# Chunked attention into a token-mixing MLP on one core: v loaded by pairs of tokens, with the odd tokens copied on chip

## The chip, the core and the metric

The kernel runs on one core of a Trainium2 chip. Five engines work beside each other, each through its own instructions in order: TensorE (PE in the profile; its weight loads are PEld), VectorE (DVE), ScalarE (ACT), GpSimd (POOL) and SyncE (SP), which here only issues transfers. 16 DMA engines move data between the chip's memory and the on-chip buffer SBUF. TensorE writes its results to PSUM, eight banks of 512 float32 per partition. The metric is the device time of one execution in microseconds; lower is better.

## The reference

Attention runs inside chunks of 64 tokens: 8 batches, 8 heads, 576 tokens, head size 64, all float32. Its output, with the heads side by side as 512 features, goes through a token-mixing MLP.

```
s = q_c @ k_c^T / 8 ;  attn = softmax(s) ;  a = attn @ v_c       # per (batch, head, chunk of 64)
x = a.transpose(0, 2, 1, 3).reshape(8, 576, 512)
wq, wk = x @ w_q, x @ w_k                                        # 512 -> 64 each
mixed = (wq @ wk^T / 8) @ x                                      # per batch, over its 576 tokens
out = relu(mixed) @ w_out                                        # float32, (8, 576, 512)
```

Since `(wq @ wk^T) @ x = wq @ (wk^T @ x)`, the kernel computes the 64 by 512 matrix `wk^T @ x` and no 576 by 576 one.

## The kernel before

The work is a list of words, `ORDER`. A loop over it calls one small function for each word, and so every engine's queue holds its instructions in the order of the words. The list is written out by hand or by a planner outside the kernel; nothing reorders it. The framework adds the waits between engines. `@n` names a PSUM bank, `:A`, `:D` or `:P` the engine (ScalarE, VectorE, GpSimd).

**Loading.** q and k are seen as 36 units of 1,024 rows (a row is one token of one head). In a unit, each of the 128 partitions holds 8 rows that follow one another, so a partition gets one run of 512 elements, 2,048 bytes read and 1,024 written as float16. A word `LDk.9_14` loads k of units 9 to 13 to all partitions, and `LDq1.9_14` the quarter of q that goes to the 32 partitions from 32 x 1. Each quarter of q has one of two slots, and the other slot stays zero (`MZ` clears it, once), so that one matmul can mix the two. q and k share a ring of 27 units (`RING`), which later also holds the output tiles on their way out (`held`). `LDv.32` loads all of v of batch 3: partition p holds token p of each 128 tokens, so each token is one run of 64 elements, 256 bytes read and 128 written. All these loads convert to float16 and are issued by GpSimd (lines 134, 142, 146), in the order of the words. `LW` loads `w_out` there too; `LS` loads the small weights through SyncE.

**One unit pair.** `TR` transposes k and q of one or two units in 32 by 32 blocks on VectorE (lines 208 and 212), `SC` computes the scores transposed, k's tokens on the partitions (line 227), and `EX` the exponentials on ScalarE, into `est`. There are 20 such steps: 16 of two units, 4 of one.

**One batch.** `PVb.p`, p = 0, 1, 2, multiplies `est` by v (line 262); v has a column of ones (`MO`), so the sums of the exponentials come with it. `RN` is a reciprocal and a multiplication on VectorE (272, 273), `XT` transposes on TensorE (283) and `XE` copies the result, `PJ` projects to wq and wk (309) and `EP` copies, `DU` duplicates a half on chip, `WT` transposes wk (336) and `EW` copies, `GM` computes `wk^T @ x` (363) and `EG` copies, `MXb.m`, m = 0 to 3, multiplies by wq (381) and `RL` applies the relu. The eight batches are finished in pairs: two batches are nine tiles of 128 tokens, each an `OM` with `w_out` (420), 36 in all, and an `OE` that copies to SBUF (432 on VectorE, 434 on ScalarE). `ST` stores tiles by SyncE (439). The first store waits for the load that `HOLD` names, so that stores don't compete with loads. `ZZn` is n matmuls on constant data (449), placed where TensorE has nothing else.

The functions that the change touches follow, as they were.

Of the kernel before, what the change touches and what calls it, by code (L numbers as in the profile page):

```python
# [17 lines left out]
MU MZ2_5_2:A MO2 LDq1.0_2 ZZ4@0 LDk.2_5 LDq2.0_2 MZ0_2_3:A LDq3.0_2 MZ0_2_0:A MZ2_5_1:D ZZ4@1 MZ2_5_0:A MZ0_2_2:A MO0  # L18
MZ5_9_9:D MO1 LDq0.0_2 LDk.0_2 LS LDq0.2_5 MO3 MZ0_2_1:A LDq3.2_5 LDq1.2_5 LDq2.2_5 MO4 MZ9_14_9:D TR0 ZZ4@0 SC0@0
MZ2_5_3:A LDv.02 TR1 EX0 LDk.5_9 LDq3.5_9 TR2 SC1@2 LDq0.5_9 SC2@0 EX1 LI EX2 LK MZ23_27_9:P PV0.0@0 LDq1.5_9 PV0.2@2  # L20
MZ14_18_9:D RN0.0 RN0.2 LDq2.5_9 PV0.1@4 ZZ4@6 LDq1.9_14 LDv.12 XT0.0@0 LDq3.9_14 XE0.0:A LDq2.9_14 ZZ4@6 RN0.1
MZ18_23_9:P XT0.1@4 TR4 XE0.1:A TR3 SC4@0 PJ0@4 EP0:D SC3@2 WT0@4 EX4 EX3 EW0:A PV1.2@2 PV1.0@0 ZZ4@4 GM0@5 LDq0.9_14
DU0:A RN1.2 PV1.1@2 ZZ4@4 EG0:A RN1.0 MX0.1@0 RN1.1 MX0.3@4 MX0.2@6 RL0.1:A XT1.0@2 RL0.2:A LDk.9_14 XT1.1@0 TR6
XE1.0:A MX0.0@6 LDv.22 ZZ4@2 SC6@2 RL0.0:A XE1.1:A PJ1@0 LW LDk.14_18 EX6 TR5 LDq1.14_18 LDq2.14_18 SC5@2 LDq3.14_18
EP1:A TR7 WT1@0 EX5 EW1:D SC7@6 DU1:D LDq0.14_18 GM1@0 EX7 RL0.3:A PV2.1@6 PV2.2@2 EG1:A LDq1.18_23 RN2.1 OM2@4 OE2:A
MX1.1@0 RN2.2 RL1.1:A MX1.0@6 PV2.0@4 MX1.2@0 RL1.0:A XT2.1@2 RL1.2:A MX1.3@6 RN2.0 XT2.0@4 XE2.1:D XE2.0:A LDq2.18_23
OM0@5 PJ2@3 TR9 OM3@2 LDq3.18_23 SC9@0 EP2:A TR8 EX9 OE0:A OE3:A LDk.18_23 WT2@3 DU2:A OM4@4 EW2:A LDq0.18_23 SC8@0
LDv.32 LDk.23_27 EX8 RL1.3:D OM6@6 OE6:A OE4:D GM2@3 EG2:A LDq0.23_27 OM8@0 MX2.0@3 RL2.0:A TR11 MX2.3@6 RL2.3:D
MX2.1@1 LDq3.23_27 OM5@5 PV3.0@6 RL2.1:A OE8:A PV3.1@0 MX2.2@2 TR12 RN3.0 OE5:A RL2.2:A LDq2.23_27 OM7@5 PV3.2@2
SC11@6 OE7:A SC12@4 EX11 RN3.1 XT3.0@0 LDq1.23_27 RN3.2 LDv.42 OM9@1 TR10 XT3.1@2 XE3.0:A OE9:A OM1@0 XE3.1:A PJ3@2  # L30
EX12 SC10@4 TR14 EP3:A DU3:D EX10 WT3@2 PV4.0@4 EW3:A PV4.1@2 PV4.2@6 LDq3.29_32 GM3@1 LDq1.29_32 OE1:A LDq2.29_32
# [525 lines left out]
```

The loads in their order are these. `LDv.12` is batch 1, all of it (the last digit, 2, means both halves).

```
LDq1.0_2 LDk.2_5 LDq2.0_2 LDq3.0_2 LDq0.0_2 LDk.0_2 LDq0.2_5 LDq3.2_5 LDq1.2_5 LDq2.2_5 LDv.02 LDk.5_9 LDq3.5_9
LDq0.5_9 LDq1.5_9 LDq2.5_9 LDq1.9_14 LDv.12 LDq3.9_14 LDq2.9_14 LDq0.9_14 LDk.9_14 LDv.22 LW LDk.14_18 LDq1.14_18
LDq2.14_18 LDq3.14_18 LDq0.14_18 LDq1.18_23 LDq2.18_23 LDq3.18_23 LDk.18_23 LDq0.18_23 LDv.32 LDk.23_27 LDq0.23_27
LDq3.23_27 LDq2.23_27 LDq1.23_27 LDv.42 LDq3.29_32 LDq1.29_32 LDq2.29_32 LDk.29_32 LDq3.27_29 LDq0.29_32 LDq2.27_29
LDq1.27_29 LDv.52 LDq0.32_36 LDq1.32_36 LDq3.32_36 LDq0.27_29 LDq2.32_36 LDk.27_29 LDk.32_36 LDv.62 LDv.72
```

And the order from the first step that uses v of batch 6:

```
PV6.0@1 OM14@5 EW5:A PV6.1@6 SC18@3 RN6.0 PV6.2@1 OE14:A RN6.1 GM5@5 XT6.0@0 EX18 RN6.2 OM19@3 XT6.1@1 EG5:D LDv.72
DU5:A XE6.0:D MX5.1@4 XE6.1:A MX5.3@6 OM20@0 PJ6@1 RL5.3:A ST0.6 TR19 SC19@6 RL5.1:A OE20:D EP6:D OM18@0 WT6@1 MX5.2@4
EX19 OE19:D EW6:D MX5.0@6 PV7.0@2 GM6@1 OE18:A RL5.2:A PV7.1@4 DU6:D RN7.0 RL5.0:A EG6:D PV7.2@6 OM22@0 RN7.2 OM26@1
OE22:A RN7.1 ST1.0 OM24@0 MX6.0@6 MX6.1@2 XT7.1@4 OE26:A ST0.3 XE7.1:A OE24:D XT7.0@0 OM25@1 RL6.1:D RL6.0:A MX6.3@4
XE7.0:D ST2.0 RL6.3:D ST1.6 OE25:A MX6.2@2 ST1.3 PJ7@6 RL6.2:A EP7:A OM28@2 WT7@6 OM29@7 ST0.0 EW7:D OE29:A DU7:A
OE28:D GM7@6 EG7:A OM27@2 OE27:A MX7.3@6 MX7.0@3 MX7.2@0 RL7.2:A RL7.0:D OM21@5 MX7.1@0 RL7.3:A RL7.1:A OM23@3 ST2.6
OE21:A OM31@0 OE23:D OM32@5 OE31:D OM30@3 OM35@0 ST3.0 OE32:D OE30:A OM34@3 ST2.3 OE34:D ST3.3 ST3.7 OM33@5 OE35:D
OE33:D ST3.8 ST3.6
```

## Time and profile before

| | |
|---|---|
| median of 3 runs | 122.64 us (121.91 to 123.4) |
| the profiled execution | 122.64 us, span of its instructions 120.8 us |
| busy: TensorE / VectorE / ScalarE / GpSimd | 98.1 / 91.9 / 72.3 / 50.2 us |
| loads that GpSimd issues | 47,536 packets, 14.68 MB written |
| read from memory / written to it | 29.62 MB / 9.44 MB |

How to read it: times are from the first instruction. A group's row has the line, the engine, the operation, output and inputs, then busy time and the mean in ns, then the idle time before and what ended it. In the chain of waits each row is a start, a length, and what the end of the kernel hung on then. In a row of a timeline the bracket holds the idle time before and its releaser. The row of a stretch gives its length, busy time and instructions of PE, PEld, DVE, ACT and POOL, the granted clock of TensorE, the mean share of the DMA engines (over 1 where packets overlap) and the GB/s written.

### The profile page before, as it was taken

The numbers are of one execution on the slowest core, as the hardware profiler recorded it, in microseconds if no ns is written. First come the engines' busy times: TensorE is split into PE (matmuls) and PEld (weight loads), VectorE is DVE, ScalarE is ACT, GpSimd is POOL, SyncE is SP. The second block draws the span as 40 slices with busy tenths as digits, with TensorE's granted clock in tenths as the row PEclk, the third lists the DMA queues.
The fourth block names the chain that finished last, engine by engine and source line by source line (L and its number), as shares of the span: only waits on it lengthen the run. The fifth ranks groups of instructions, "written<-read, shape, count | busy, mean of one in ns | idle before, by whom it ended". The sixth has DMA issues, their size and how long they took to land.

```text
span 120.8 us, 3838 instructions
## 1 busy us (share of the span) xinstructions
PE 98.1 (81%) x1664; PEld 55.1 (46%) x1664; DVE 91.9 (76%) x131; ACT 72.3 (60%) x117; POOL 50.2 (42%) x68
## 2 busy tenths in 40 slices
...
GB/s 8 120 196 157 167 205 203 171 179 205 178 175 207 202 203 200 180 172 205 176 172 204 96 157 193 209 171 157 137 156 401 234 351 423 417 123 260 260 362 159
DMA packets 50144, 24.62 MB, mean 204 GB/s; under 512 B 38096, under 2 KB 48336, under 8 KB 50128
## 3 DMA queue, kind: packets, MB, share of 16 engines
q0 software_dynamic: 47536, 14.68, 112.8%
...
q14 instruction: 3, 0.02, 0.0%
HBM read 29.62 MB, written 9.44 MB: 323 GB/s over the span
## 4 chain that ended last, share of the span: by engine, by line
DMA 59%; PE 24%; POOL 7%; issue 5%; DVE 1%; DVEq 0%; POOLq 0%
DMA qk<-in_k_dram 32%; DMA vt<-in_v_dram 27%; PE pb L420 14%; PE pb L363 2%; PE pb L262 2%; POOL qk L146 2%; PE pb L283 2%; POOL qk L153 2%; POOL vt L134 2%; PE pb L381 2%; PE pb L309 2%; DVE qk L432 1%; PE pb L227 1%; POOL qk L142 1%; PE pb L336 1%
## 5 line engine op out<-in xcount | busy, mean ns | idle before, releaser
L420 PE MATMUL pb<-wout,rmx 128*128 128x512 f16 x144 | 35.8, 381 | 0.1
L146 POOL DMA_DIRECT2D qk<-in_q_dram x40 | 22.3, 563 | 20.7 <-DMA vt<-in_v_dram 9.2
L239 ACT ACTIVATE est<-pb 128x1024 f16<-128x1024 f32 (+1 forms) x20 | 18.6, 939 | 12.4 <-PE pb L227 12.4
L273 DVE TENSOR_TENSOR xn<-pb,rec 128x768 f16<-128x768 f32 x24 | 23.0, 958 | 1.0 <-DVE rec L272 0.2
L212 DVE STREAM_TRANSPOSE qT<-qk 128x1024 f32<-128x1024 f32 (+1 forms) x20 | 22.1, 1105 | 1.2 <-DMA qk<-in_q_dram 1.2
L208 DVE STREAM_TRANSPOSE kT<-qk 128x512 f32<-128x512 f32 (+1 forms) x20 | 20.1, 1004 | 2.8 <-DMA qk<-in_k_dram 2.4
L227 PE MATMUL pb<-qT,kT 64*64 64x128 f16 x576 | 12.8, 229 | 8.4 <-DVE qT L212 8.3
L434 ACT COPY qk<-pb 128x512 f32<-128x512 f32 x24 | 13.9, 590 | 8.9 <-PE pb L420 7.9
L420 PEld LDWEIGHTS <-rmx 128*128 128x128 f16 x144 | 13.3, 103 | 12.2 <-issue 0.7
L397 ACT ACTIVATE rmx<-pb 128x576 f16<-128x576 f32 x25 | 15.4, 657 | 2.7 <-PE pb L381 2.6
L134 POOL DMA_DIRECT2D vt<-in_v_dram x8 | 14.8, 1847 | 5.0 <-PE pb L262 3.4
L227 PEld LDWEIGHTS <-kT 64*64 64x64 f16 x576 | 10.2, 112 | 11.2 <-DVE kT L208 4.9
L262 PE MATMUL pb<-vt,est 64*64 64x65 f16 x576 | 8.5, 200 | 6.7 <-DMA vt<-in_v_dram 5.3
L299 ACT COPY xT<-pb 128x768 f32<-128x768 f32 (+1 forms) x13 | 8.5, 651 | 7.7 <-PE pb L283 7.7
L449 PE MATMUL pb<-unit 128*128 128x512 f16 x32 | 11.7, 520 | 1.5 <-DVE unit L465 1.5
L283 PE MATMUL pb<-iden,xn 128*128 128x128 f32 x72 | 11.3, 294 | 0.4 <-DVE xn L273 0.2
L262 PEld LDWEIGHTS <-est 64*64 64x64 f16 x576 | 7.1, 112 | 9.5 <-DMA vt<-in_v_dram 4.4
L272 DVE RECIPROCAL rec<-pb 128x12 f32<-128x12 f32 x24 | 5.4, 227 | 7.4 <-PE pb L262 6.1
L432 DVE COPY qk<-pb 128x512 f32<-128x512 f32 x12 | 8.1, 685 | 3.9 <-PE pb L420 3.7
L283 PEld LDWEIGHTS pb<-iden,xn 128*128 128x128 f32 x72 | 8.8, 151 | 3.4 <-DVE xn L273 1.4
L309 PE MATMUL pb<-xT,wpj 128*128 128x512 f16 (+1 forms) x48 | 9.0, 323 | 0.0
L142 POOL DMA_DIRECT2D qk<-in_k_dram x10 | 7.8, 784 | 2.3 <-DMA qk<-in_k_dram 2.3
...
## 6 DMA issues: line engine op xcount, KB each, us to landing
...
```

What stands on the lines that cost most here:

```text
L134: return nc.gpsimd.dma_start(vt[b % NV][:, lo:hi, 0:D], flat[2][b * H * S : (b + 1) * H * S].rearrange("(c p) d -> p c d", p=P)[:, lo:hi],)
L146: return nc.gpsimd.dma_start(x[rows, 1 + i % 2], runs[0][rows, lo:hi])
L208: nc.vector.transpose(out=kT[x % NQ][:, 0:n].bitcast(F32).rearrange("p u (x r) o -> p u r (x o)", r=R), in_=src[:, 0],)
L212: nc.vector.transpose(out=qT[x % NQ][:, :, 0:n].bitcast(F32).rearrange("p s u r x o -> p s (u r) (x o)"), in_=src[:, 1:3].rearrange("p s u ...
L227: nc.tensor.matmul(ps[CH * o : CH * o + CH, bank + f, at : at + P], lhsT=kT[x % NQ][rows, u, CH * j : CH * j + CH, e], rhs=qT[x % NQ][rows ...
L239: nc.scalar.activation(est[x % NE][:, 0 : 8 * n].rearrange("p m (w r) -> p m w r", r=R), src.rearrange("p (m r w) -> p m w r", r=R, w=R), ...
L262: nc.tensor.matmul(ps[CH * o : CH * o + CH, bank + (n + o) % 2, at : at + D + 1], lhsT=est[x % NE][rows, 4 * size * g + 4 * u + 2 * (j // ...
L273: nc.vector.tensor_tensor(out=xn[b % 3][:, 3 * p : 3 * p + 3].rearrange("p t (f i) d -> p i (t f) d", f=2), in0=xv[:, :, :, 0:D], in1=rec[ ...
L283: nc.tensor.transpose(ps[:, bank + at // 4, P * (at % 4) : P * (at % 4) + P], xn[b % 3][:, i].rearrange("p h c -> p (h c)").bitcast(F32), ...
L397: nc.scalar.activation(dst, src, AF.Relu, scale=scale_moe)
L420: nc.tensor.matmul(ps[:, bank, :], lhsT=c[:, r], rhs=wout[:, i, :], start=(i == 0), stop=(i == NI - 1),)
L434: nc.scalar.copy(os_, ps[:, bank, :])
```

## The change

v of a batch is loaded in two halves, `LDv0.b` and `LDv1.b`: v0 holds the first 64 of each 128 tokens, v1 the others. The 64 tokens are taken as 32 pairs; partition i of 32 gets tokens 2i and 2i + 1 as one run of 128 elements, 512 bytes read and 256 written. `VMb.f` then copies the odd tokens of half f of batch b from these 32 partitions to the next 32, on GpSimd (15 times) or VectorE (once). In each 64 rows of v the even tokens so come first and the odd ones behind, and k's transpose puts its tokens in that order: it is two instructions now, one for each parity. The column of ones moves to the front. v has 3 buffers and not 5.

The ring of q and k has 18 units and not 27, with fewer and longer first and last pieces; the output tiles of the first pair of batches, and three of the second, get a tile of their own (`osb`). `RN` becomes `RC` and `RM`, two words. `ZZ` has 44 matmuls and not 32. The whole order is new. Loads and copies in it:

```
LDq2.0_5 LDq1.0_5 LDq3.0_5 LDq0.0_5 LDq3.5_9 LDk.0_2 LDq1.5_9 LDk.2_5 LDq2.5_9 LDq0.5_9 LDk.5_9 LDv0.0 LDv1.0 LDv1.1
LDv0.1 LDk.9_14 LDq1.9_14 LDq3.9_14 VM0.0:P VM0.1:P VM1.1:P VM1.0:P LDq0.9_14 LDq2.9_14 LDv0.2 LDq1.14_18 LDk.14_18
LDq2.14_18 LDq0.14_18 LDq3.14_18 LDv1.2 LW VM2.0:P LDv0.3 LDv1.3 LDq3.18_23 VM2.1:P LDq1.18_23 LDk.18_23 LDq2.18_23
LDq0.18_23 VM3.1:P LDq1.23_27 LDq3.23_27 VM3.0:D LDv1.4 LDq0.23_27 LDk.23_27 LDq2.23_27 LDv0.4 LDq3.27_32 LDv0.5
LDv1.5 LDq2.27_32 VM4.1:P LDq0.27_32 LDk.27_32 VM4.0:P LDq1.27_32 LDq3.32_36 VM5.0:P VM5.1:P LDq0.32_36 LDv1.6
LDq2.32_36 LDq1.32_36 LDk.32_36 LDv0.6 LDv1.7 VM6.1:P VM6.0:P LDv0.7 VM7.1:P VM7.0:P
```

From the first step that uses v of batch 6:

```
PV6.2@4 RL4.3:A TR18 SC19@2 RC6.2 EG5:A EX19 PV6.1@0 RM6.2 OM20@7 OE15:A RC6.1 SC18@2 RM6.1 PV6.0@5 OM18@4 LDv0.7
DU5:A MX5.0@0 VM7.1:P EX18 OE20:A RC6.0 RM6.0 RL5.0:A MX5.2@2 OE18:D XT6.0@5 VM7.0:P RL5.2:A PV7.0@6 XT6.1@0 XE6.0:A
XE6.1:A ST0.3 PV7.1@2 PV7.2@4 RC7.0 RM7.0 XT7.0@6 RC7.2 PJ6@0 XE7.0:A ST1.0 RC7.1 RM7.2 EP6:A OM19@4 RM7.1 MX5.1@0
MX5.3@2 WT6@5 XT7.1@6 RL5.1:D RL5.3:A EW6:D DU6:A OM22@2 XE7.1:A OM23@5 PJ7@6 OE22:A EP7:A OE19:D DU7:D OM25@2 WT7@6
OE25:A EW7:D ST2.0 OE23:A GM6@7 EG6:A GM7@6 MX6.1@4 RL6.1:A MX6.0@2 EG7:D MX6.3@0 OM21@7 RL6.0:D RL6.3:A ST1.3 OE21:A
MX7.0@2 MX7.3@4 RL7.0:D MX7.2@0 ST0.0 OM26@6 MX7.1@2 RL7.3:A ST2.3 RL7.2:A MX6.2@4 OM24@7 RL7.1:D RL6.2:A OM30@2
OM32@3 OM31@4 OM27@5 ST1.6 OE26:D OM28@6 OE31:A OM29@4 OE24:D OM34@7 OM33@0 OE32:A OE30:D OE27:D OE28:A ST2.6 OE29:A
OE33:D OM35@4 ST3.3 ST3.0 OE34:A ST3.7 OE35:A ST3.6 ST3.8
```

The diff without the order's text:

```diff
 
-HOLD = "v.72"
+HOLD = "v1.7"
 AHEAD = "k.0_2"
 
 
@@ -73,16 +75,16 @@
     NPR = NG // 4
     NI = DM // P
     HS = S // 2
-    VP = 72
+    VP = 130
     VO = D + 2
     R = 8
     NU = B * H * S // (P * R)
-    RING = 27
+    RING = 18
     UNITS = []
     for a in range(0, NU, 9):
         UNITS += [(a, a + 2), (a + 2, a + 4), (a + 4, a + 5), (a + 5, a + 7), (a + 7, a + 9)]
     of_unit = {u: (x, u - lo) for x, (lo, hi) in enumerate(UNITS) for u in range(lo, hi)}
-    NV = 5
+    NV = 3
     NQ = 3
     NE = 5
     scale_attn = 1.0 / math.sqrt(D)
@@ -93,7 +95,7 @@
     ctx.enter_context(tc.manual_schedule())
 
     RD = R * D
-    PIECES = [(0, 2), (2, 5), (5, 9), (9, 14), (14, 18), (18, 23), (23, 27), (27, 29), (29, 32), (32, 36)]
+    PIECES = [(0, 5), (5, 9), (9, 14), (14, 18), (18, 23), (23, 27), (27, 32), (32, 36)]
     qk = sb.tile([P, RING * 3 * RD], F16, name="qk")
 
     def piece(u):
@@ -105,7 +107,7 @@
     kT = [sb.tile([P, 2, 32 * R, 2], F16, name=f"kT{i}") for i in range(NQ)]
     qT = [sb.tile([P, 2, 2, R, 32, 2], F16, name=f"qT{i}") for i in range(NQ)]
     est = [sb.tile([P, 16, CH], F16, name=f"est{i}") for i in range(NE)]
-    rec = [sb.tile([P, 2, 6], F32, name=f"rec{i}") for i in range(3)]
+    rec = [[sb.tile([P, 2, 6], F32, name=f"rec{j}{i}") for i in range(3)] for j in range(2)]
     xn = [sb.tile([P, NPR, 4, D], F16, name=f"xn{i}") for i in range(3)]
     xT = [sb.tile([P, NPR, P, 2], F16, name=f"xT{i}") for i in range(2)]
     wqk = [sb.tile([P, S], F16, name=f"wqk{i}") for i in range(4)]
@@ -117,6 +119,7 @@
     wpj = sb.tile([P, 2, 2, 2 * DH], F16, name="wpj")
     wpl = sb.tile([P, 2, 2 * DH], F16, name="wpl")
     wout = sb.tile([P, NI, DM], F16, name="wout")
+    osb = sb.tile([P, 12 * DM], F32, name="osb")
     ident = sb.tile([P, P], F16, name="ident")
     iden4 = sb.tile([P, P], F32, name="iden4")
     unit = sb.tile([P, 512], F16, name="unit")
@@ -129,11 +132,13 @@
     def load(word):
         it, _, rng = word.partition(".")
         if it[0] == "v":
-            b, f = int(rng[0]), int(rng[1])
-            lo, hi = (0, NG) if f == 2 else (NG // 2 * f, NG // 2 * f + NG // 2)
+            b, f = int(rng), int(it[1])
+            rows = slice(CH * f, CH * f + CH // 2)
             return nc.gpsimd.dma_start(
-                vt[b % NV][:, lo:hi, 0:D],
-                flat[2][b * H * S : (b + 1) * H * S].rearrange("(c p) d -> p c d", p=P)[:, lo:hi],
+                vt[b % NV][rows, :, 2 : 2 + 2 * D],
+                flat[2][b * H * S : (b + 1) * H * S].rearrange(
+                    "(g f i o) d -> f i g (o d)", f=2, i=CH // 2, o=2
+                )[f],
             )
         lo, hi = (int(x) for x in rng.split("_"))
         first, n, x = piece(lo)
@@ -149,8 +154,17 @@
         lo, hi, part = (int(x) for x in word.split("_"))
         n, x = piece(lo)[1:]
         if part == 9:
-            e = nc.vector if eng == "D" else nc.gpsimd
-            e.memset(x[:, n * RD :].bitcast(F32), 0.0)
+            to = x[:, n * RD :].bitcast(F32)
+            if eng == "A":
+                nc.scalar.activation(
+                    to.rearrange("p (u w) -> p u w", w=RD // 2),
+                    unit[:].bitcast(F32)[:, None].broadcast_to([P, 2 * n, RD // 2]),
+                    AF.Copy,
+                    scale=0.0,
+                )
+            else:
+                e = nc.vector if eng == "D" else nc.gpsimd
+                e.memset(to, 0.0)
             return
         rows = slice(32 * part, 32 * part + 32)
         slot = 2 - part % 2
@@ -198,6 +212,15 @@
         make_identity(nc, iden4[:])
         nc.gpsimd.tensor_copy(ident[:], iden4[:])
 
+    def vm(b, f, eng):
+        x = vt[b % NV].bitcast(I32)
+        half = CH // 2
+        lo = CH * f
+        e = nc.vector if eng == "D" else nc.gpsimd
+        e.tensor_copy(
+            x[lo + half : lo + CH, :, 1 : 1 + D // 2], x[lo : lo + half, :, 1 + D // 2 : 1 + D]
+        )
+
     def tr(x):
         lo, hi = UNITS[x]
         first, m, src = piece(lo)
@@ -205,10 +228,11 @@
         src = src.bitcast(F32).rearrange("p (s u r w) -> p s u r w", s=3, u=m, w=32)[
             :, :, lo - first : hi - first
         ]
-        nc.vector.transpose(
-            out=kT[x % NQ][:, 0:n].bitcast(F32).rearrange("p u (x r) o -> p u r (x o)", r=R),
-            in_=src[:, 0],
-        )
+        to = kT[x % NQ][:, 0:n].bitcast(F32)
+        to = to.rearrange("p u (X o l r) z -> p o r (u X) (l z)", X=4, o=2, l=R)
+        of_k = src[:, 0].rearrange("p u (r o) w -> p o r u w", o=2)
+        for o in range(2):
+            nc.vector.transpose(out=to[:, o], in_=of_k[:, o])
         nc.vector.transpose(
             out=qT[x % NQ][:, :, 0:n].bitcast(F32).rearrange("p s u r x o -> p s (u r) (x o)"),
             in_=src[:, 1:3].rearrange("p s u r w -> p s (u r) w"),
@@ -262,18 +286,22 @@
                         nc.tensor.matmul(
                             ps[CH * o : CH * o + CH, bank + (n + o) % 2, at : at + D + 1],
                             lhsT=est[x % NE][rows, 4 * size * g + 4 * u + 2 * (j // 2) + pi],
-                            rhs=vt[b % NV][rows, n // 2, 0 : D + 1],
+                            rhs=vt[b % NV][rows, n // 2, 1 : D + 2],
                             start=True,
                             stop=True,
                         )
 
-    def rn(b, p, bank):
-        xv = ps[:, bank : bank + 2, 0 : 6 * VO].rearrange("p k (n d) -> p k n d", n=6)
-        nc.vector.reciprocal(rec[p][:], xv[:, :, :, D])
+    def values(bank):
+        return ps[:, bank : bank + 2, 0 : 6 * VO].rearrange("p k (n d) -> p k n d", n=6)
+
+    def rc(b, p, bank):
+        nc.vector.reciprocal(rec[b % 2][p][:], values(bank)[:, :, :, 0])
+
+    def rm(b, p, bank):
         nc.vector.tensor_tensor(
             out=xn[b % 3][:, 3 * p : 3 * p + 3].rearrange("p t (f i) d -> p i (t f) d", f=2),
-            in0=xv[:, :, :, 0:D],
-            in1=rec[p][:, :, :, None].broadcast_to([P, 2, 6, D]),
+            in0=values(bank)[:, :, :, 1 : D + 1],
+            in1=rec[b % 2][p][:, :, :, None].broadcast_to([P, 2, 6, D]),
             op=ALU.mult,
         )
 
@@ -325,7 +353,8 @@
         if eng == "A":
             nc.scalar.copy(wq2[b % 4][CH:P], wqk[b % 4][0:CH])
         else:
-            nc.vector.tensor_copy(wq2[b % 4][CH:P], wqk[b % 4][0:CH])
+            e = nc.vector if eng == "D" else nc.gpsimd
+            e.tensor_copy(wq2[b % 4][CH:P], wqk[b % 4][0:CH])
 
     def wt(b, bank):
         t16 = ps[:, bank, :].bitcast(F16)
@@ -397,11 +426,12 @@
             nc.scalar.activation(dst, src, AF.Relu, scale=scale_moe)
 
     of = out.rearrange("b s m -> (b s) m")
-    OB = (9, 15, 21, 0)
-
     def held(pr, at, size):
-        lo = OB[pr] * 3 * RD + at * 2 * DM
-        return qk[:, lo : lo + size * 2 * DM].bitcast(F32)
+        if pr == 0 or pr == 1 and at < 3:
+            lo = at * DM + pr * NCH * DM
+            return osb[:, lo : lo + size * DM]
+        lo = {1: -3, 2: 6, 3: 15}[pr] + at
+        return qk[:, lo * 2 * DM : (lo + size) * 2 * DM].bitcast(F32)
 
     GROUPS = [[3, 3, 3], [3, 3, 3], [3, 3, 3], [3, 3, 1, 1, 1]]
 
@@ -465,7 +495,7 @@
             nc.vector.memset(unit[:], 1.0)
             continue
         if kind == "MO":
-            nc.vector.memset(vt[int(rest)][:, :, D : D + 1], 1.0)
+            nc.vector.memset(vt[int(rest)][:, :, 1:2], 1.0)
             continue
         if kind == "LW":
             weights()
@@ -488,12 +518,16 @@
             tr(n)
         elif kind == "SC":
             sc(n, banks["SC", n, 0])
+        elif kind == "VM":
+            vm(n, x, eng)
         elif kind == "EX":
             ex(n, banks["SC", n, 0])
         elif kind == "PV":
             pv(n, x, banks["PV", n, x])
-        elif kind == "RN":
-            rn(n, x, banks["PV", n, x])
+        elif kind == "RC":
+            rc(n, x, banks["PV", n, x])
+        elif kind == "RM":
+            rm(n, x, banks["PV", n, x])
         elif kind == "XT":
             xt(n, x, banks["XT", n, x])
         elif kind == "XE":
```

56 lines of the change are left out of this document (29 added, 27 removed).

## The prediction

> **What bounds the kernel now.** I read the page first, then the chain of waits in order of time, then stretches of the run, the GpSimd timeline and the groups by shape.
>
> ```profile
> span 120.8 us, 3838 instructions
> PE 98.1 (81%) x1664; PEld 55.1 (46%) x1664; DVE 91.9 (76%) x131; ACT 72.3 (60%) x117; POOL 50.2 (42%) x68
> ...
> GB/s 8 120 196 157 167 205 203 171 179 205 178 175 207 202 203 200 180 172 205 176 172 204 96 157 193 209 171 157 137 156 401 234 351 423 417 123 260 260 362 159
> ...
> q0 software_dynamic: 47536, 14.68, 112.8%
> ...
> DMA 59%; PE 24%; POOL 7%; issue 5%; DVE 1%; DVEq 0%; POOLq 0%
> ```
>
> The chain is 59% transfers, and nearly all the rest is TensorE. In order of time:
>
> ```profile
> 27.52 14.76 DMA qk<-in_k_dram
> ...
> 42.57 7.56 DMA qk<-in_k_dram
> ...
> 50.42 14.26 DMA vt<-in_v_dram
> ...
> 74.92 10.25 DMA vt<-in_v_dram
> ...
> 85.21 0.38 PE pb L262 x24
> ...
> 86.57 0.31 PE pb L262 x23
> ...
> 87.46 1.09 issue
> ...
> 92.94 1.02 PE pb L309 x8
> 93.97 0.58 PE pb L227 x29
> ...
> 100.84 1.13 PE pb L283 x9
> ...
> 102.84 0.35 PE pb L381 x4
> 103.19 1.13 PE pb L309 x8
> ...
> 105.19 0.37 PE pb L336 x6
> ...
> 106.53 0.79 PE pb L363 x10
> ...
> 110.04 5.31 PE pb L420 x24
> 115.35 0.02 issue
> 115.37 1.29 DVE qk L432 x2
> ```
>
> Loads set the pace until v of batch 6 lands at 85.17. From its first matmul, 85.21, TensorE runs to 115.35 with 1.09 idle, so 29.05 us of work. In the written order PV6.0 to the end is 6 PV, 2 pairs of units of SC, 4 XT, 2 PJ, 2 WT, 3 GM, 12 MX and 19 OM. At the rows' prices (PV 0.34, between its two rows; SC 0.58; XT 1.13 a pair; PJ 1.08, the mean of its two rows; WT 0.37; GM 0.79; MX 0.35; OM 5.31/6 = 0.885) this is 31.75. Steps overlap at their ends, so I scale every sum of this kind by 29.05/31.75 = 0.915.
>
> So a release at time T of a step with work W behind it ends TensorE no earlier than T + W. For PV6.0 that is 85.21 + 29.05 = 114.3, and the real end is 1.1 later. Earlier releases have slack:
>
> ```profile
> 28.28 0.58 PE L262 MATMUL pb<-vt,est 64*64 64x65 f16 x48 [1.12 <-DMA vt<-in_v_dram]
> 28.80 1.04 PE L449 MATMUL pb<-unit 128*128 128x512 f16 x4
> ```
>
> PV1.2 starts at 28.28 with 85.5 x 0.915 = 78.3 behind it (21 PV, 13.5 SC, 14 XT, 7 PJ, 7 WT, 8 GM, 32 MX, 36 OM, and 12 matmuls of ZZ at 0.26): 106.6. v of batch 4 lands at 64.7 (50.42 + 14.26) with 52.1 x 0.915 = 47.7 behind PV4.0: 112.4. So the bound rises from load to load: transfers are slower than the work they feed, and the last ones set the end. After TensorE come 5.45 us of copies, the last stores and the finish. The profiled execution took 122.64 us, 1.84 over its span, and is the median of the three runs.
>
> **Transfers.** Two stretches, the columns ending in the granted clock, DMA share and GB/s written:
>
> ```profile
> 42.50:48.00 5.50, 5.43 (x67) 3.15 (x66) 5.30 (x8) 2.27 (x5) 5.43 (x7) 1.00 1.24 201
> 80.00:84.00 4.00, 4.00 (x56) 1.89 (x55) 3.62 (x6) 3.75 (x7) 0.00 (x0) 1.00 2.43 158
> ```
>
> The first holds only q and k, packets of 1,024 B written; the second only v, packets of 128 B. A unit of q or of k (131,072 B) costs 0.65 us, wout 2.6, a batch of v (589,824 B) 3.73. Per packet that is 5.09 ns and 0.81 ns. A line through both gives 1.42 ns at 256 B, so a batch of v in 2,304 packets costs 3.27, a half-batch load 1.64. The bounds are 1.87 (no faster per byte) and 1.47 (as fast as q). I take 1.64, the line through both rows; the saving is 8 x 0.46 = 3.7 us of transfer.
>
> A rule that speaks against the change: the Trainium skill, "SBUF — State Buffer", section "Door 1: The DMA port swizzle", says that 32 partitions from 0 reach 8 of 16 ports, with 189 GB/s measured at 1 MiB against 328 for all; the new v loads write 32 partitions each. By that page's figure a half (294,912 B) would take an estimated 1.56 us, not more than my 1.64, so the rule alone would not undo the gain. The row of 42.5 to 48 is the case in point: from k's landing at 42.3 seven q loads of 32 partitions each are next in the queue, and 201 GB/s were written. So 32 partitions are no limit at the 180 GB/s that 1.64 us means.
>
> When a load lands is the sum of the loads ahead of it in the order plus an offset for start, the weights' transfers, latency and stalls. Batch 4 of v: 54 units 35.1, wout 2.6, five batches 18.7, sum 56.4; it landed at 64.7, offset 8.3. Batch 1: 19.25 units and two batches, 20.0, 28.28: 8.3 too. Batch 6: 75.5, offset 9.7. I use 8.3.
>
> **GpSimd.** It issues all these loads in order, and now also copies.
>
> ```profile
> 1.30 0.66 POOL L146 DMA_DIRECT2D qk<-in_q_dram  x1 [0.86 <-POOLq L541]
> ...
> 12.18 0.29 POOL L199 CAST ident<-iden 128x128 f16<-128x128 f32 x1
> 12.41 1.80 POOL L153 MEMSET qk<- 128x2048 f32 x1
> ...
> 33.65 0.57 POOL L146 DMA_DIRECT2D qk<-in_q_dram  x1 [2.56 <-DMA qk<-in_k_dram]
> 37.19 0.57 POOL L146 DMA_DIRECT2D qk<-in_q_dram  x1 [2.96 <-DMA vt<-in_v_dram]
> 39.69 0.57 POOL L146 DMA_DIRECT2D qk<-in_q_dram  x1 [1.94 <-DMA wout<-in_moe_w_out_dram]
> 42.57 0.86 POOL L142 DMA_DIRECT2D qk<-in_k_dram  x1 [2.31 <-DMA qk<-in_k_dram]
> ```
>
> The issue at 39.69 waits for wout and the one at 42.57 for k of 14 to 18: each for the load eight before it. The window stays eight while loads shrink, yet eight q loads still hold 5.2 us. The queue now also stands still at each copy (VM) until its half has landed: behind it wait the later loads, and DMA runs dry if what was issued ahead is used up first. From the order, the stock behind the awaited half is 4.9 us at VM1.0 (k, q1, q3 of 9 to 14), 6.7 at VM2.1, 6.5 at VM3.1, 6.3 at VM5.1, but at VM6.0 only v1.7, 1.64. Only there do I count a gap.
>
> A copy moves 32 x 1,152 words. By the memset row it is 1.0 us (0.88 ns a word), by the cast row taken whole per element 2.6. The cast is mostly fixed time, so I take 1.3, near the memset. Fifteen make 19.5 us; two memsets like the row's 1.80 go. Contention with VectorE could only cost; a memset writes and does not read, so no row shows a copy's. The issue of a half of v I put at 0.95, between these:
>
> ```profile
> L146 POOL DMA_DIRECT2D qk<-in_q_dram x40 | 22.3, 563 | 20.7 <-DMA vt<-in_v_dram 9.2 <-DMA qk<-in_k_dram 7.7 <-DMA wout<-in_moe_w_out_dram 1.9
> L134 POOL DMA_DIRECT2D vt<-in_v_dram x8 | 14.8, 1847 | 5.0 <-PE pb L262 3.4 <-DMA qk<-in_k_dram 1.6
> ```
>
> **The other edits.** k's transposes become two of half the size.
>
> ```profile
> 13.49 0.61 DVE L208 STREAM_TRANSPOSE kT<-qk 128x256 f32<-128x256 f32 x1
> 13.94 0.69 DVE L212 STREAM_TRANSPOSE qT<-qk 128x512 f32<-128x512 f32 x1
> ...
> 44.59 1.11 DVE L208 STREAM_TRANSPOSE kT<-qk 128x512 f32<-128x512 f32 x1
> 45.55 1.20 DVE L212 STREAM_TRANSPOSE qT<-qk 128x1024 f32<-128x1024 f32 x1
> ```
>
> From start to start a full one takes 0.96, a half 0.45, so two cost 0.90: between -1.2 us over all 20 by these and +2.2 by the durations (0.61 x 2 against 1.11); I take nothing, since spacing is what an engine in a row pays. VectorE, busy 91.9 us, also gives two EP, two OE, one RL and one XE to ScalarE (busy 72.3) and takes one copy, so it stays below TensorE's 98.1, and either end hides there. The ring of 18 makes a load wait for the transposes of 18 units earlier, some 25 us of loads ago: no cost; the split reciprocal only lets other words stand between its halves. The column of ones shifts the operands of PV and RM by one element: by the shapes at most 1/65 of each, for PV 24 x 0.34 / 65 = 0.1 us in all, taken as nothing. Of the 44 ZZ (1.04/4 = 0.26 each) 12 lie behind PV1.0 and are in its work. Nor do stores bind: they are let go at v1.7 instead of v of batch 7.
>
> **The sum.** Landing, 1.3 for the copy, then the work behind it:
> - PV1.0: v0.1 after 18 units and 4 halves, 18.3 + 8.3 = 26.5; 27.8 + 88.1 x 0.915 = 108.4 (21 PV, 13.5 SC, 16 XT, 8 each of PJ, WT, GM, 32 MX, 36 OM, 12 ZZ).
> - PV2.2: v1.2 after 36 units, 6 halves, 33.2; 42.8 + 66.6 = 109.4 (18 PV, 10 SC, 12 XT, 6 each, 25 MX, 36 OM).
> - PV4.0: v0.4 after 54 units, wout, 10 halves, 54.1; 63.7 + 46.0 = 109.7 (12 PV, 5.5 SC, 8 XT, 4 each, 16 MX, 27 OM).
> - PV5.0: v1.5 after 55.25 units, wout, 12 halves, 58.2; 67.8 + 42.1 = 109.9 (9 PV, 4.5 SC, 8 XT, 4 each, 16 MX, 24 OM).
> - PV6.2: v0.6 after 72 units, wout, 14 halves, 72.4; 82.0 + 27.5 = 109.5 (6 PV, 2 SC, 4 XT, 2 PJ, 2 WT, 2 GM, 12 MX, 18 OM).
> - PV7.0: v0.7 is issued only after VM6.0 at 82.0: 0.95, an estimated 1.0 to the first bytes (the first issue ends at 1.96, and by 3.02 the first slice had moved 8 GB/s x 3.02 = 24 KB), 1.64 and 1.3 make 86.9; + 22.75 = 109.6 (3 PV, 3 XT, 2 PJ, 2 WT, 2 GM, 10 MX, 16 OM).
>
> The late releases gain 4.4 us and the early ones lose their slack. TensorE's end: 109.9, plus the 1.1 that the old kernel lost after its last release, plus 0.5 because six releases now lie within 1.5 us: 111.5. The tail loses some copying:
>
> ```profile
> L434 ACT COPY qk<-pb 128x512 f32<-128x512 f32 x24 | 13.9, 590 | 8.9 <-PE pb L420 7.9
> ```
>
> The last two copies were one after the other on VectorE, 1.29; the last is now a single one on ScalarE, 0.59: 5.45 - 0.7 = 4.75. Span 116.25, time 118.1.
>
> **Rivals.**
> - *v no faster per byte* (1.87 a half). For: packets stay small. Against: 1,024 B packets do better. PV7.0 comes 15 x 0.23 = 3.4 later, 113.0: time 121.2.
> - *As fast as q* (1.47): PV5.0 2.0 earlier, PV1.0 0.7; then 108.0 binds: about 116.
> - *Slower: GpSimd becomes the bound.* From v0.0's landing (21.6) it has 13 copies and 40 issues (22 q at 0.57, 5 k and wout at 0.86, 12 of v at 0.95: 29.1) before v0.7 moves. PV7.0 starts at 21.6 + 29.1 + 2.6 + 14c; TensorE ends 22.75 + 1.6 later, 77.7 + 14c for a copy of c. At 1.3 that is 95.9 and binds nothing; at the cast's 2.6, 114.1, time 120.7; over 1% slower from c = 2.85, and 126 at 3.0. For: reads with a stride, a shared queue. Against: the memset row.
> - *No slack left*: each of six releases passes on 0.5 us more: 121.1. For: the sums above. Against: the old kernel, with three late releases within 2 us, lost 1.1.
>
> **The numbers.** Forecast 0.58; v no faster 0.13; as fast as q 0.09; GpSimd 0.10; no slack 0.10. About 1% is what a measurement of this kernel can tell from no change: 121.4 and 123.9. Faster: 0.56 of the forecast, 0.09, and over half of each of the two cases at 121: 0.77. Slower: GpSimd and a little of the others, 0.11. Same: 0.12. Range 115.4 to 121.8: it holds all but GpSimd's case, part of the two at 121 and 0.04 below.
>
> **What would show it.** v packets of 256 B, 18,432, and above 158 GB/s in stretches with v alone; copies of 1.0 to 1.6 us; v0.6 near 81; the chain's last transfer before 87; TensorE's end near 111.5. A chain through GpSimd's copies, or DMA slices far below 150 GB/s before 80 us, would prove me wrong.

## The result and the profile after

The changed kernel takes 129.57 us, the median of 4 runs (127.78 to 130.21), against 122.79 (121.91 to 123.4) before: **1.047 times the time before, with a 95% interval of 1.032 to 1.062**. The forecast was 118.1, faster. Ratios here and below leave disturbed executions out, so they are not quite the quotient of the medians, and the profiled execution of after, 129.92 us, is one of its longer ones.

The page of after, its lines that answer to those shown of before:

```profile
span 128.1 us, 3880 instructions
PE 101.4 (79%) x1676; PEld 57.1 (45%) x1676; DVE 87.1 (68%) x143; ACT 74.5 (58%) x120; POOL 57.2 (45%) x80
...
PEclk9997579869999999999999999999995589999998
...
GB/s 6 162 150 184 206 200 182 178 201 139 122 175 189 201 184 198 205 188 173 189 187 199 209 171 177 180 74 217 264 345 13 0 0 257 418 243 405 394 372 129
...
q0 software_dynamic: 29088, 14.68, 89.3%
...
DMA 39%; PE 27%; issue 15%; POOL 13%; ACT 1%; POOLq 1%
```

The packets fell as planned: 47,536 - 29,088 = 18,448 fewer. But the clock row (PEclk, the granted clock of TensorE in tenths of full speed) shows two slices at 5 near the end (slices of 3.2 us, these from 96 to 102.5), and there the rate is next to nothing: 13, 0, 0. The old kernel has no such hole; there TensorE ran on from 85.2, with 1.09 us idle. The end of the chain of waits of after:

```profile
58.18 12.08 DMA vt<-in_v_dram
...
86.32 0.76 POOL vt L137
87.12 1.17 POOL vt L220
88.30 8.11 issue
96.41 1.19 POOLq L586
97.64 0.55 PE pb L286 x22
...
114.36 8.76 PE pb L450 x40
123.14 0.59 ACT qk L464
```

The 8.11 us called "issue" are a wait for a load. GpSimd's timeline of after says which:

```profile
85.15 1.17 POOL L220 COPY vt<-vt 32x1152 int32<-32x1152 int32 x1 [5.74 <-DMA vt<-in_v_dram]
86.27 0.81 POOL L137 DMA_DIRECT2D vt<-in_v_dram  x1
87.12 1.17 POOL L220 COPY vt<-vt 32x1152 int32<-32x1152 int32 x1
96.43 1.16 POOL L220 COPY vt<-vt 32x1152 int32<-32x1152 int32 x1 [8.13 <-DMA vt<-in_v_dram]
```

v0.7, the last half, is issued at 86.27 and is there at 96.38, just before its copy starts: 10.1 us for a load whose data alone are 1.6 us at the prediction's price. Beside it stand the first stores, in SyncE's timeline of after, and the rate in 40 slices of 0.4 us from 84 to 100:

```profile
86.41 2.04 SPq L469 DMA_DIRECT2D out_dram<-osb  x3
```

```profile
GB/s 154 61 51 13 11 0 0 0 445 292 323 215 215 215 205 104 158 237 221 404 358 415 339 426 312 413 403 421 348 147 16 31 15 0 0 0 0 41 0 0
```

`HOLD = "v1.7"` lets the stores go when v1.7 lands, 86.33. In the new order v0.7 is behind v1.7, and its issue has only just begun, 0.06 us before. Three stores of 768 KB (2.36 MB) go out from 86.41, beside 0.29 MB of v0.7. The transfers by queue, from 87 to 96 (packets, MB, share of the 16 engines; q1 has the stores, q0 the loads):

```profile
q1 hardware_dynamic: 426, 2.33, 76.7%
q0 software_dynamic: 1166, 0.29, 32.8%
```

In these 9 us a store's packet holds an engine for 0.767 x 16 x 9 / 426 = 0.26 us, one of v for 0.04: the stores take most of the time of the engines that v needs. The first packet of v0.7 moves only at 89.8, 3.5 us after its issue, and from 92 to 96 the load queue moves 266 packets beside 250 of the stores, about one for one. The Trainium skill, "DMA: Bandwidth & Descriptors", section "Queues, rings and completion order", says that each DMA engine takes its queues in turn, a packet at a time, a packet there being several descriptors. The trace agrees in kind: both queues move at once, about one for one where both are at work (the 1,166 to 426 of the whole stretch include 1.5 us in which the stores nearly pause).

### The profile page after: what moved, and what is told of

The parts are those of the page before. It is cut to its first block, busy times and chain, and to the rows that moved or that the text cites. A ratio compares the mean times of both kernels' runs of the same rounds, so it can differ in the third digit from the quotient of the medians.

```text
span 128.1 us, 3880 instructions
## 1 busy us (share of the span) xinstructions
PE 101.4 (79%) x1676; PEld 57.1 (45%) x1676; DVE 87.1 (68%) x143; ACT 74.5 (58%) x120; POOL 57.2 (45%) x80
## 3 DMA queue, kind: packets, MB, share of 16 engines
q0 software_dynamic: 29088, 14.68, 89.3%
## 4 chain that ended last, share of the span: by engine, by line
DMA 39%; PE 27%; issue 15%; POOL 13%; ACT 1%; POOLq 1%
DMA vt<-in_v_dram 35%; PE pb L450 15%; POOL vt L220 5%; DMA qk<-in_q_dram 4%; POOL qk L151 4%; POOL vt L137 3%; PE pb L311 3%; PE pb L337 3%; PE pb L286 2%; PE pb L410 1%; PE pb L392 1%; POOLq L586 1%; POOL qk L147 1%; ACT rmx L426 1%; PE pb L365 0%
## 5 line engine op out<-in xcount | busy, mean ns | idle before, releaser
L220 POOL COPY vt<-vt 32x1152 int32<-32x1152 int32 x15 | 17.7, 1180 | 31.7 <-DMA vt<-in_v_dram 31.7
L235 DVE STREAM_TRANSPOSE kT<-qk 128x256 f32<-128x256 f32 (+1 forms) x40 | 19.6, 566 | 5.6 <-DMA qk<-in_k_dram 5.6
L151 POOL DMA_DIRECT2D qk<-in_q_dram x32 | 18.1, 570 | 4.2 <-DMA qk<-in_k_dram 2.7
L426 ACT ACTIVATE rmx<-pb 128x576 f16<-128x576 f32 x26 | 16.3, 664 | 2.8 <-PE pb L410 2.5
L286 PE MATMUL pb<-vt,est 64*64 64x65 f16 x576 | 9.4, 204 | 9.3 <-POOL vt L220 8.3
L479 PE MATMUL pb<-unit 128*128 128x512 f16 x44 | 14.4, 466 | 1.5 <-DVE unit L495 1.5
L464 ACT COPY qk<-pb 128x512 f32<-128x512 f32 x17 | 9.8, 588 | 6.6 <-PE pb L450 6.5
L137 POOL DMA_DIRECT2D vt<-in_v_dram x16 | 13.1, 821 | 1.0 <-DMA qk<-in_k_dram 0.6
L337 PE MATMUL pb<-xT,wpj 128*128 128x512 f16 (+1 forms) x48 | 9.9, 345 | 1.3 <-ACT xT L327 1.2
L350 ACT CAST wqk<-pb 128x576 f16<-128x576 f32 x8 | 5.1, 640 | 7.9 <-PE pb L337 7.9
```

The costliest lines, as they stand in the source:

```text
L137: return nc.gpsimd.dma_start(vt[b % NV][rows, :, 2 : 2 + 2 * D], flat[2][b * H * S : (b + 1) * H * S].rearrange("(g f i o) d -> f i g (o d ...
L151: return nc.gpsimd.dma_start(x[rows, 1 + i % 2], runs[0][rows, lo:hi])
L220: e.tensor_copy(x[lo + half : lo + CH, :, 1 : 1 + D // 2], x[lo : lo + half, :, 1 + D // 2 : 1 + D])
L235: nc.vector.transpose(out=to[:, o], in_=of_k[:, o])
L286: nc.tensor.matmul(ps[CH * o : CH * o + CH, bank + (n + o) % 2, at : at + D + 1], lhsT=est[x % NE][rows, 4 * size * g + 4 * u + 2 * (j // ...
L426: nc.scalar.activation(dst, src, AF.Relu, scale=scale_moe)
```

## The experiments

The theories, with the letters of the expectations where these use them. A: the stores, released before the last load has moved, share the DMA engines with it, and this is the loss. B: the rival of A that each expectation names, such as a half that is slow by itself. C: GpSimd stands at the copy VM1.0 while DMA runs dry, and so every later load is late. D: there is no slack, TensorE's work behind the releases is larger than I had put it. E: with the loads in time TensorE itself binds. F: the ZZ matmuls only fill time in which TensorE waits anyway.

**1. The stores held for the last load.** The first store's word also moves behind the copy VM7.1, as the load that it waits for must stand ahead of it.

```diff
-HOLD = "v1.7"
+HOLD = "v0.7"
-LDv1.7 ST0.6 EX15 VM6.1:P
+LDv1.7 EX15 VM6.1:P
-LDv0.7 DU5:A MX5.0@0 VM7.1:P EX18
+LDv0.7 DU5:A MX5.0@0 VM7.1:P ST0.6 EX18
```

> The changed kernel, but the first store waits for the last half of v (v0.7) and not for v1.7. Theory A (the last half is slowed because the first three stores, released 0.1 us after its issue, share the DMA engines with it packet by packet): v0.7 lands 2.5 to 4 us after its issue and not 10.1, so near 89 to 90; TensorE's end comes 6 to 9 us earlier, time 121 to 123. Rival B (v0.7 is slow by itself, because it is issued alone into an empty queue behind GpSimd's copy): it still lands 8 us or more after its issue and the time stays at 128 to 130.

Measured: 121.58 us, ratio to before 0.990 (0.981 to 0.999). GpSimd's timeline of this kernel, and its rates in 40 slices from 84 to 95:

```profile
83.10 1.17 POOL L220 COPY vt<-vt 32x1152 int32<-32x1152 int32 x1 [4.69 <-DMA vt<-in_v_dram]
84.22 0.81 POOL L137 DMA_DIRECT2D vt<-in_v_dram  x1
85.08 1.17 POOL L220 COPY vt<-vt 32x1152 int32<-32x1152 int32 x1
88.98 1.16 POOL L220 COPY vt<-vt 32x1152 int32<-32x1152 int32 x1 [2.74 <-DMA vt<-in_v_dram]
```

```profile
GB/s 0 0 0 0 0 0 28 19 13 61 139 186 184 181 161 98 63 0 0 0 0 357 357 492 447 424 380 380 380 380 469 424 402 424 380 358 492 424 424 402
```

The same load, alone: issued 84.22, landed 88.93, 4.7 us and not 10.1 (A had put 2.5 to 4). Its first packet moves 1.5 us after the issue and not 3.5, and its packets take 2.7 us and not 6.2. Only then do the stores start, at above 350 GB/s. A is confirmed, and B, by which the half would still take 8 us, is out: what the first store waits for turns 4.7% slower into about 1% faster. TensorE ends at 113.84 against 123.12. Of these 9.28 us, 5.4 are the load, 2.05 lie ahead of it (in the profiled execution of after the issue came that much later, before any store, so this isn't the edit's), and 1.8 come behind it. TensorE's timeline of this kernel has PV7.0 at

```profile
90.61 0.38 PE L286 MATMUL pb<-vt,est 64*64 64x65 f16 x24
```

without a wait, and 23.2 us of work behind it; in after the same work took 25.5 (97.64 to 123.12), with a granted clock of 0.50 from 97.64 to 102.5; half of these 4.9 us is about the difference.

**2. The last half issued earlier, the stores as they were.**

```diff
-LDv1.7 ST0.6 EX15 VM6.1:P
+LDv1.7 LDv0.7 ST0.6 EX15 VM6.1:P
-LDv0.7 DU5:A
+DU5:A
```

> The changed kernel, but LDv0.7 is issued right behind LDv1.7, ahead of the copies VM6.1 and VM6.0; the stores still wait for v1.7 alone. Theory A: v0.7's packets follow v1.7's without a gap and are nearly all through when the first store's packets begin, so it lands at 88 to 89; time 120 to 122. Rival B expects the same here; a theory that blames the work behind PV7.0 alone (order too tight, cold clock) expects 127 or more.

Measured: 123.43 us, ratio 1.001 (0.995 to 1.006). v0.7 lands at 86.07, 1.5 us behind v1.7; it was in the queue before the stores, which start at 84.62. So the other way of taking the collision away works too, which speaks for A again. But A's time of 120 to 122 missed: it gains less than edit 1, though the load is 2.9 us earlier. TensorE's timeline of this kernel has a gap of that size:

```profile
92.22 0.32 PE L286 MATMUL pb<-vt,est 64*64 64x65 f16 x15
94.23 0.45 PE L286 MATMUL pb<-vt,est 64*64 64x65 f16 x33 [1.69 <-issue]
```

A gap of 1.69 us in the middle of a PV, released by nothing that the profile shows. In that stretch the other engines and DMA are nearly still as well:

```profile
92.50:94.20 1.70, 0.04 (x6) 0.00 (x0) 0.33 (x1) 0.63 (x1) 0.00 (x0) 1.00 0.00 0
```

Its cause was not settled, and with one trace it is not shown that the gap is the whole difference; the last section has what the traces say of it.

**3. Both.** Edits 1 and 2 together.

> Both edits: LDv0.7 right behind LDv1.7, and the first store waits for v0.7. Theory A: v0.7 lands near 88, no store beside it; time 119.5 to 121.5, at most 1 us under the one with the early load alone. What then is still missing to my 118.1 would be the 4 us by which v0.6 landed later (85.1, forecast 80.7).

Measured: 122.61 us, ratio 0.988 (0.982 to 0.994); span 119.7, v0.7 landed at 87.73. The median lies above the 119.5 to 121.5 expected, but the ratio is not to be told from edit 1's: with the collision gone, 1.2 us of the last load are worth nothing.

**4 and 7. The same collision made in the old kernel.** The old kernel holds its stores for its last load. Released one batch earlier, and two:

```diff
-HOLD = "v.72"
+HOLD = "v.62"
```

> The kernel before, but its first store waits for v of batch 6 and not of batch 7, so that stores run beside the last load of v as they do in the changed kernel. Theory A: v of batch 7, which landed 3.5 us after batch 6, now lands 8 to 14 us after it (93 to 99), because each of its packets waits for a store's; its PV7.0 has about 19.4 us of TensorE's work behind it, so the time rises by 0 to 4 us. Rival B: the landing stays within 5 us of batch 6's and the time does not change.

```diff
-HOLD = "v.72"
+HOLD = "v.52"
```

> The kernel before, but the first store waits for v of batch 5 (lands at 74.4), so that three stores of 768 KB run beside the last q, k and v loads. Theory A (a store beside loads takes their packets' turns one for one): the loads that were to land from 75 to 85 land up to 6 us later, batch 6 near 89 to 91 and not 85.2, and the time rises by 2 to 6 us to 125 to 129. Rival B (stores fill idle time of the engines): batch 6 lands within 2 us of before and the time stays or falls.

Measured: 122.82 us, ratio 0.997 (0.993 to 1.002), for the first, where the last batch landed about 3.5 us after batch 6, as in the old kernel (85.17 and 88.65): the stores are issued from 85.62, their first packet moves at 86.8, and by then all but 607 of the 4,608 packets of a batch were through. A's number for it missed, and the run says little on the collision, because there was hardly one. The second took 128.78 us (median of four, 126.18 to 132.04), where before took 122.93 on the same chip; four scattered executions give no ratio, but the lowest of them is 3.2 us above that median. SyncE's and TensorE's timelines of the second:

```profile
74.30 7.86 SPq L439 DMA_DIRECT2D out_dram<-qk  x3
```

```profile
90.67 0.55 PE L262 MATMUL pb<-vt,est 64*64 64x65 f16 x24 [6.41 <-DMA vt<-in_v_dram]
```

Batch 6 lands at 90.63 where it landed at 85.17; A had put 89 to 91, B within 2 us. The queues of this kernel from 82 to 85 us, with almost no store moving, and from 86 to 89 (packets, MB, share of the 16 engines):

```profile
q0 software_dynamic: 3657, 0.47, 244.5%
```

```profile
q1 hardware_dynamic: 198, 1.12, 95.2%
q0 software_dynamic: 199, 0.03, 12.9%
```

Beside the stores the loads fall from 3,657 packets in 3 us to 199, one for each packet of the stores, and nearly all of these are 48 times as long (6,144 bytes against 128). So the loss needs neither the pairs nor the new order, only stores that start ahead of loads that are still to move. As far as a run can, this shows A's mechanism by itself.

**5. Loads issued ahead of the copies** (on top of edit 1), so that GpSimd doesn't stand at VM1.0 with nothing issued.

```diff
-LDq3.9_14 VM0.0:P ZZ4@2 EX0 TR2 SC1@1 VM0.1:P VM1.1:P
+LDq3.9_14 LDq0.9_14 LDq2.9_14 VM0.0:P ZZ4@2 EX0 TR2 SC1@1 VM0.1:P LDv0.2 VM1.1:P
-ZZ2@0 VM1.0:P EX1 LDq0.9_14 LDq2.9_14 PV0.1@0
+ZZ2@0 LDq1.14_18 VM1.0:P EX1 PV0.1@0
```

> The changed kernel with the first store held for v0.7, and with four early loads issued ahead of copies that GpSimd waits for: q0 and q2 of units 9 to 13 before VM0.0, v0.2 before VM1.1, q1 of 14 to 17 before VM1.0. Theory C (the loads came 2 to 4 us late because GpSimd stood at VM1.0 until v0.1 had landed and issued nothing, so that the DMA engines ran nearly dry from 28 to 36 us): the GB/s of that stretch rise from 127 to 170 towards 180 to 200, v1.2 lands near 40 and not at 42.7, v0.6 near 80.5 and not at 83.1, and the time falls 1 to 3 us below the 121.6 of the held kernel, to 118.5 to 120.5. Rival D (after 60 us the engines' own order binds, not the loads): the loads come earlier and the time stays within 1 us of 121.6.

Measured: 121.77 us, ratio 0.987 (0.979 to 0.995): the time of edit 1. Stretches of before, of after, of edit 1 and of this kernel (columns as in the prediction):

```profile
28.00:36.00 8.00, 7.12 (x145) 4.05 (x146) 6.26 (x9) 4.06 (x8) 3.05 (x6) 1.00 1.80 182
...
60.00:80.00 20.00, 17.54 (x389) 10.86 (x388) 17.46 (x26) 14.12 (x24) 11.04 (x13) 1.00 1.58 172
```

```profile
28.00:36.00 8.00, 6.06 (x135) 4.31 (x125) 7.10 (x13) 6.39 (x12) 7.18 (x12) 0.99 1.11 139
```

```profile
28.00:36.00 8.00, 6.88 (x86) 4.57 (x83) 7.60 (x15) 5.14 (x10) 7.29 (x11) 1.00 1.23 154
36.00:60.00 24.00, 22.61 (x449) 13.11 (x446) 20.59 (x34) 16.59 (x28) 14.95 (x21) 1.00 1.39 188
60.00:80.00 20.00, 19.30 (x400) 11.37 (x399) 18.61 (x34) 17.05 (x31) 12.06 (x16) 1.00 1.45 195
80.00:90.00 10.00, 9.86 (x232) 5.71 (x230) 7.83 (x14) 9.94 (x18) 4.12 (x4) 1.00 0.89 94
90.00:113.84 23.84, 23.73 (x226) 12.11 (x224) 12.00 (x21) 14.76 (x26) 0.15 (x1) 1.00 0.86 347
```

```profile
28.00:36.00 8.00, 7.31 (x107) 4.80 (x95) 7.83 (x16) 5.16 (x10) 4.75 (x8) 1.00 1.37 200
36.00:60.00 24.00, 23.15 (x466) 13.37 (x470) 20.96 (x37) 17.11 (x30) 16.11 (x22) 1.00 1.39 185
```

C's mechanism is right: 200 GB/s instead of 154, and v0.7 lands at 87.48, 1.45 us earlier. But no time that the runs can tell goes with it (C had put 118.5 to 120.5). The third block says what is the bound then: in edit 1's kernel TensorE is busy for 75.5 of the 77.84 us from 36 to its end. In the old kernel it lost 2.5 of 20 us between 60 and 80, where its chain ran through v; here 0.7. Loads no longer set the pace. That is D; how much of "busy" is needed, experiment 8 asks.

**8. The ZZ behind PV1.0 left out** (on top of edit 5). The 12 matmuls compute nothing that is used.

```diff
-DU0:A XE1.0:D ZZ2@6 WT0@2
+DU0:A XE1.0:D WT0@2
...
-ZZ4@4 LDq2.18_23
+LDq2.18_23
```

(so too ZZ2 behind WT1 and GM1 and before SC9)

> The kernel with the held store and the early issues, without the twelve filler matmuls (ZZ) behind PV1.0, which compute nothing. Theory E (with the loads in time TensorE itself binds from PV1.0 to the end, in order): its end comes 2 to 3 us earlier (12 x 0.22 to 0.26 us), time 118.5 to 120 against 121.8. Rival F (the loads still bind behind PV2.2): the matmuls only filled waiting time, the time stays within 1 us of 121.8, and TensorE shows 2 to 3 us of idle time between 28 and 44 us.

Measured: 122.29 us, ratio 0.994 (0.990 to 0.998). The stretch from 36 to 60, and the longest gap in TensorE's timeline there:

```profile
36.00:60.00 24.00, 21.57 (x448) 13.45 (x446) 22.43 (x38) 17.20 (x29) 15.82 (x22) 1.00 1.38 180
```

```profile
42.50 0.28 PE L410 MATMUL pb<-wqk,g 64*128 64x288 f16 x1 [1.05 <-ACT est L263]
```

Work of about 3 us is gone, and the time is not, so E is out: TensorE's own queue isn't the bound there. F's number came, though not F's reason in the expectation, that loads bind. None of TensorE's waits from 28 to 44 us is for a load; the longest, the row shown, is for ScalarE's exponentials. TensorE's "busy" was padded; under it VectorE is at 22.43 of 24 us. So what holds the middle of the kernel looks like the chain over VectorE, ScalarE and TensorE, not one queue of matmuls; no run took work out of VectorE or ScalarE to show it.

**6 and 9. Edit 1's order without the pairs.** First v by halves of 64 partitions, packets of 128 B written, no copies, k's transpose whole; then v by whole batches over 128 partitions, each at the place of the half that came first.

```diff
-            rows = slice(CH * f, CH * f + CH // 2)
...
-                vt[b % NV][rows, :, 2 : 2 + 2 * D],
...
+            rows = slice(CH * f, CH * f + CH)
...
+                vt[b % NV][rows, :, 2 : 2 + D],
```

> The changed order with the first store held for v0.7, but v's halves loaded token by token (128 B written, 64 partitions), no copies, and k's transpose in one instruction as before. This undoes the pairs alone. By my sum each half costs 0.23 us more (1.87 instead of 1.64), 3.4 us by the last one; against that GpSimd no longer stands at the copies and a half can be used 1.2 us after landing earlier, and v0.7 isn't issued behind a copy. Theory (pairs give little net): within 1.5 us of the held kernel's 121.6. Rival (pairs are the gain): 123.5 or more.

```diff
-                vt[b % NV][rows, :, 2 : 2 + D],
+                vt[b % NV][:, :, 2 : 2 + D],
```

> The changed order with the first store held for the last v load, no copies, k's transpose whole, and v loaded as in the kernel before: one load of 128 partitions a batch, packets of 128 B, in place of the first of its two halves. With the run that kept halves of 64 partitions it tells the pairs from the halves. If the halves were the cost there (119 GB/s in a stretch with v alone, where whole batches made 158), the batch takes 3.7 to 3.8 us again and the time is 121.5 to 123.5, between the held kernel (121.6) and the halves without pairs (127.0). If the pairs' lower packet count is the whole difference, it stays at 125 or more.

Measured: 126.97 us, ratio 1.025 (1.019 to 1.032), and 125.14 us, ratio 1.015 (1.010 to 1.021). I had expected the halves within 1.5 us of edit 1 and was wrong; of the two cases for the whole batches, it came out as the one at 125 or more. Where v moves almost alone in the kernel of halves, in an execution of 131.08 us, a stretch shows:

```profile
20.00:24.00 4.00, 1.33 (x35) 0.70 (x36) 2.46 (x3) 1.02 (x1) 0.57 (x1) 1.00 4.51 119
```

119 GB/s, where whole batches over 128 partitions had 158 in the old kernel with the same packets, and pairs over 32 partitions 174 to 183. The Trainium skill, "SBUF — State Buffer", section "Door 1: The DMA port swizzle", gives a range of 64 partitions from 0 no more ports than 32, 8 of 16. This row agrees in direction, 64 partitions are slower than 128, though by a quarter; and another stretch of the same execution with v alone, from 86.5 to 92, has 147 GB/s, so the size of it is open. Against whole batches in this order the pairs are worth 2.5% (0.990 against 1.015). That isn't all transfer: GpSimd's issues of v there wait for TensorE for 7.0 us (10.9 in the kernel of halves, nothing in edit 1's), in an order that was laid out for halves and copies. That v moves faster in pairs is shown by the rates; what share of the 2.5% is theirs is not.

**10. Edit 8 with edit 2's place for the last half**, a try at the best of all.

```diff
-LDv1.7 EX15
+LDv1.7 LDv0.7 EX15
```

> As without the late filler, and the last half of v issued right behind v1.7, ahead of the copies VM6.1 and VM6.0, so that it doesn't wait for them. Theory E: TensorE binds, so this adds less than 0.7 us to what the filler's removal gives: 118 to 120. If a load still binds at the end, it adds 1 to 2 us.

Measured: 123.39 us, ratio 0.996 (0.991 to 1.001), a miss. TensorE's timeline shows the gap of edit 2 again, with v0.7 landed at 85.41:

```profile
94.17 0.36 PE L286 MATMUL pb<-vt,est 64*64 64x65 f16 x21 [1.31 <-issue]
```

No version gained on edits 1, 3 and 5, which are not to be told apart: about 1% under the old kernel, 5.5% under the changed one (0.990 / 1.047).

## Why the prediction was wrong

**The step that failed** is the sentence "Nor do stores bind: they are let go at v1.7 instead of v of batch 7". It cost the edit of `HOLD` at nothing, and it compared the wrong things. In the old kernel v of batch 7 is the last load of all, so nothing is left for stores to meet; v1.7 is the last but one. The prediction had both halves of the answer: it issued v0.7 "only after VM6.0 at 82.0" and gave it 1.0 + 1.64 us behind the issue, with v1.7 already landed by then. One line more, "what else is released when v1.7 lands", would have set 2.36 MB of stores beside a load of 0.29 MB that ends the kernel. The sum for PV7.0 said 86.9; it started at 97.64. Of these 10.7 us, 4.3 came before the load (VM6.0 ended at 86.27, not 82.0) and 6.5 in it (10.1 from issue to landing, not 3.6); the copy was as forecast. Of the 6.5, 5.4 are the stores; 1.1 stay without them, as the half alone took 4.7 us: its packets moved in 2.7 us and not in 1.64. Behind it TensorE's work took 25.5 us and not 22.75, at half its clock for the first 4.9. The tail was right: 4.98 us after TensorE's end, 4.75 forecast.

**The second miss, some 3 us, is the size of W**, the work behind a release. With the collision gone the time is 121.58, still 3.5 above the forecast. PV2.2's row in edit 1's kernel:

```profile
43.94 0.38 PE L286 MATMUL pb<-vt,est 64*64 64x65 f16 x23 [0.71 <-POOL vt L220]
```

From 43.94 to TensorE's end at 113.84 are 69.9 us; the sum was 42.8 + 66.6. The release was 1.1 late, the work 3.3 larger; the forecast had 1.6 for such things on top of 109.9. From 43.94 on TensorE is busy for 68.5 us and idle for 1.4, so most of the 3.3 is not waiting: the sum at the prediction's prices was 72.75 before the scale cut it to 66.6, and the trace lies between. The scale of 0.915 was fitted on the end of the old kernel and was too kind for the rest; why is not shown. The list with six releases within 1.5 us said itself that little slack was left. "No slack left", 121.1 at a chance of 0.10, has the time of the mended kernel, but not its mechanism: from PV2.2 on TensorE waits there for a copy of v once, the 0.71 us of the row above, and not at six releases.

**Third, the dry queue.** "Only there do I count a gap", at VM6.0: but GpSimd, by its timeline of after, also stood at the first four copies, VM1.0 last, and between 15.85 and 28.44 issued no load:

```profile
27.32 1.17 POOL L220 COPY vt<-vt 32x1152 int32<-32x1152 int32 x1 [1.28 <-DMA vt<-in_v_dram]
28.44 1.13 POOL L151 DMA_DIRECT2D qk<-in_q_dram  x2
```

From 28 to 36 us 139 GB/s were written, against 182 before (both rows above). Loads in the middle were late (v1.2 landed at 44.4, forecast 41.5). Experiment 5 mends it and gains nothing, so in the mended kernel it is worth no time; in the changed kernel it is some part of the 4.3 us by which VM6.0 was late; 2.05 of these were not there in edit 1's kernel, which has the same loads up to there, so they are not the order's.

**What held.** v alone writes at the rate put down for it (180 GB/s), in stretches of after:

```profile
18.00:22.00 4.00, 2.87 (x43) 1.19 (x40) 3.54 (x6) 1.76 (x3) 1.17 (x1) 1.00 1.80 183
82.50:84.00 1.50, 1.50 (x51) 1.16 (x50) 0.33 (x1) 1.48 (x4) 0.00 (x0) 1.00 1.86 174
```

So the limit of 32 partitions, which the prediction weighed, did not undo it. The copies cost 1.18 us on GpSimd (1.3 forecast), an issue 0.82 (0.95), the halves of k's transposes 0.61 each:

```profile
L220 POOL COPY vt<-vt 32x1152 int32<-32x1152 int32 x15 | 17.7, 1180 | 31.7 <-DMA vt<-in_v_dram 31.7
L235 DVE STREAM_TRANSPOSE kT<-qk 128x256 f32<-128x256 f32 x32 | 17.2, 612 | 5.6 <-DMA qk<-in_k_dram 5.6
L137 POOL DMA_DIRECT2D vt<-in_v_dram x16 | 13.1, 821 | 1.0 <-DMA qk<-in_k_dram 0.6 <-PE pb L286 0.4
```

VectorE's busy time fell from 91.9 to 87.1. Of the signs that the prediction named, the packets, their rate and the copies came; v0.6 at 81 (85.1), the last transfer before 87 (96.38) and TensorE's end at 111.5 (123.12) did not. None of the four rivals was what happened: the rival on the slower side, GpSimd as the bound, needed copies of 2.85 us and got 1.18. The case that was missing from the list was one in which the order of two words, and not the price of a part, decides; the range of 115.4 to 121.8 had no room for it.
